# Top-k attention and a SmeLU MLP on one core: a PSUM bank for the values' result, weight words loaded ahead, two small VectorE operations moved, early MLP work limited

## The chip, the cores and the metric

The kernel runs on one core of one Trainium2 chip. The metric is the device time of one execution in microseconds (us); times of several runs are given as their median. All tensors are float32.

## The reference, cut to what matters

Attention in which each query keeps its 32 largest scores (B, H, S, D = 8, 8, 576, 64), then an MLP of 4608 tokens with 512 inputs, 2048 hidden units and the SmeLU activation.

```python
scores = scale * np.matmul(q, k.transpose(0, 1, 3, 2))        # scale = 1/sqrt(64)
kth = np.partition(scores, -top_k, axis=-1)[..., -top_k:-top_k + 1]
scores = np.where(scores >= kth, scores, -1e9)
attn = np.exp(scores - np.max(scores, axis=-1, keepdims=True))
attn = attn / (np.sum(attn, axis=-1, keepdims=True) + 1e-9)
x = np.matmul(attn, v)                                        # then (B, H, S, D) -> (B*S, H*D)

h = x @ w_in                                                  # 512 x 2048
g = np.where(h >= 1, h, np.where(h <= -1, 0.0, (h + 1) ** 2 / 4))
out = g @ w_out                                               # 2048 x 512
```

The weights w_in and w_out come as float64 and are turned into float32 on the chip from their two 32-bit words.

## The kernel before

**Steps.** Attention is cut into 144 steps. A step is one pair of heads of one tile of 128 queries (or, for the last 64 queries of a batch, two pairs of heads). `begin_at(m + 2)` makes the scores two steps ahead (L227 to L242: eight matmuls into four PSUM tiles `sp`, each copied by ScalarE into `s`). `weights` (L252 to L304) is VectorE's main work: `pairs` (L250) takes the larger of each two scores, four rounds of MAX8 (L264) and MATCH_REPLACE8 (L273) find the largest, L266 negates the first maximum for ScalarE's exponential (L268), L278 to L285 find the 32nd value `kth`, L286 notes in `excess` whether the pairing was safe, L295 masks and sums, L300 and L301 give the reciprocal, GpSimd scales (L303). `transpose_w` (L307) turns the weights by TensorE, `values` (L321) multiplies by v into the PSUM tile `po`, and ScalarE copies that into `xT` (L342, L344).

**MLP.** When the tokens of a chunk (one or two tiles) are complete, `mlp` (L353) puts its units on the list `pending`: 16 first products `hidden` (L360, into a PSUM tile `ph`), each followed by two ScalarE activations `r` and `g` (L364, L366) and three GpSimd operations (L367 to L369), then second products `final` (L377, into `py`) with the copy to `y` and the store. A unit of cost stands for 128 x 128 x 128; `hidden` costs 4 per tile, a `final` piece 8.

**PSUM.** Of eight banks, four are shared in turn by all tiles with the tag "a" (`pk`, `pkt`, `pq`, `sp`, `pw`, `pwt`, `po`), three by `ph`, one is `py`.

**Weights.** 64 pieces of 128 x 256 (32 of w_in, then 32 of w_out). `convert_piece` (L99) loads the words `raw`, shifts the high word on VectorE (L105, into `bits`), converts the low word on ScalarE (L108), and then, for even pieces, takes the sign on ScalarE (L111) and adds and multiplies on GpSimd (L112, L119); for odd pieces VectorE merges the sign bit by a mask (L123) and GpSimd adds (L125). Two pieces are begun before step 0, then one in each of the seven slots of a step, so steps 0 to 8 are "early". Afterwards `inspect_piece` (L128) loads each piece again, one a step, for a check on small values.

**Order.** TensorE, VectorE, ScalarE and GpSimd execute in the order in which the code emits (L456); each queue is in order. SyncE (SP) issues all DMAs in order. The planner `advance` (L441) emits pending MLP units when their share is due or when its own estimate of TensorE's time, `pe_time`, lies behind `now`; `K_TIME` (L438) is its estimate of VectorE's time for a step. A step's share is the work left over the steps left, at most what is pending over the steps until the next chunk.

**Keys.** `keys_of` (L185) loads two heads, transposes them, and yields, four times per batch; with the fourth it loads v. `judge` (L574) looks at all notes at the end; when a note is positive, everything is run again without pairing (it is not here).

Of the kernel before, what the change touches and what calls it, by code (L numbers as in the profile page):

```python
# [10 lines left out]
F32 = mybir.dt.float32  # L11
U32 = mybir.dt.uint32
I32 = mybir.dt.int32
AF = mybir.ActivationFunctionType
ALU = mybir.AluOpType
# [8 lines left out]
def kernel(  # L24
# [68 lines left out]
    def load_words(pool, i):  # L93
        raw = pool.tile([P, 2 * WC], U32, name="raw", bufs=3)
        nc.sync.dma_start(out=raw, in_=pieces_of_weights[i][1].bitcast(U32))
        words = raw.rearrange("p (n t) -> p n t", t=2)
        return words[:, :, 0], words[:, :, 1]

    def convert_piece(pool, i, any_size):  # L99

        lo, hi = load_words(pool, i)
        dst = pieces_of_weights[i][0]

        bits = pool.tile([P, WC], U32, name="bits", bufs=2)
# [4 lines left out]
        if any_size or i % 2 == 0:  # L109
            sign = pool.tile([P, WC], F32, name="sign", bufs=2)  # L110
            nc.scalar.activation(sign, hi.bitcast(F32), AF.Sign)  # L111
            nc.gpsimd.tensor_tensor(out=bits.bitcast(I32), in0=bits.bitcast(I32), in1=units.bitcast(I32), op=ALU.add)  # L112
            if any_size:
                size = pool.tile([P, WC], F32, name="units", bufs=3)
                nc.scalar.activation(size, hi.bitcast(F32), AF.Abs)
                nc.vector.scalar_tensor_tensor(out=sign, in0=size, scalar=TINY, in1=sign, op0=ALU.is_ge, op1=ALU.mult)

                nc.vector.tensor_scalar(bits.bitcast(F32), bits.bitcast(F32), LARGEST, -LARGEST, ALU.min, ALU.max)
            nc.gpsimd.tensor_tensor(out=dst, in0=sign, in1=bits.bitcast(F32), op=ALU.mult)  # L119
            yield  # L120
        else:
            yield
            nc.vector.scalar_tensor_tensor(out=units.bitcast(U32), in0=hi, scalar=0x80000000, in1=units.bitcast(U32),  # L123
                                           op0=ALU.bitwise_and, op1=ALU.bitwise_or)
            nc.gpsimd.tensor_tensor(out=dst.bitcast(I32), in0=bits.bitcast(I32), in1=units.bitcast(I32), op=ALU.add)  # L125
        yield

    def inspect_piece(pool, i):  # L128

        _, hi = load_words(pool, i)  # L130
# [6 lines left out]
    def run(ctx, paired):  # L137
# [47 lines left out]
        def keys_of(b):  # L185
# [4 lines left out]
            for hp in range(NHP):  # L190
# [3 lines left out]
                if hp == 0:  # L194
                    nc.sync.dma_start(out=k_tl, in_=k[b, :, SM:S, :].rearrange("h p d -> p h d"))
# [14 lines left out]
                if hp == NHP - 1:  # L210
                    got["v"], got["v_tl"] = load_values(b)
# [40 lines left out]
        def weights(st, after):  # L252
# [9 lines left out]
            for r in range(0, TOP_K, 8):  # L262
                for i in range(2):
                    nc.vector.max(out=tops[:, i, r:r + 8], in_=src[:, i, :])  # L264
                if r == 0:
                    nc.vector.tensor_scalar(nmax, tops[:, :, 0], -1.0, None, ALU.mult)  # L266
# [10 lines left out]
            if paired:  # L277
# [6 lines left out]
                for i in range(2):  # L284
                    nc.vector.max(out=kth[:, i, :], in_=tops[:, i, TOP_K - 1:TOP_K + 8])  # L285
                nc.vector.tensor_tensor(out=excess[:, 2 * m:2 * m + 2], in0=seconds[:, :, 7], in1=kth[:, :, 0],  # L286
                                        op=ALU.subtract)
# [14 lines left out]
            for i in range(2):  # L302
                nc.gpsimd.tensor_scalar(e[:, i, :], e[:, i, :], rz[:, i:i + 1], 1.0, ALU.mult, ALU.mult)  # L303
            yield  # L304
# [16 lines left out]
        def values(st):  # L321
            t, hp, v_in, v_tl = st["t"], st["hp"], st["keys"]["v"], st["keys"]["v_tl"]
            wT, wTt = st["wT"], st["wTt"]
            po = ps.tile([P, P], F32, name="po", tag="a", bufs=4)
# [28 lines left out]
        def mlp(xT, tiles, pool):  # L353
# [3 lines left out]
            def hidden(f):  # L357
# [10 lines left out]
                nc.gpsimd.tensor_tensor(out=r, in0=r, in1=r, op=ALU.mult)  # L368
# [51 lines left out]
        def convert():  # L420
# [5 lines left out]
            if begun < n_pieces:  # L426
                piece = convert_piece(mlp_pool, begun, not paired)
                next(piece)
                begun += 1

        def inspect():
            nonlocal inspected
            if paired and inspected < n_pieces:
                inspect_piece(mlp_pool, inspected)
                inspected += 1


        K_TIME, PIECE_TIME, UNIT_TIME, SLOTS = 9.8, 0.5, 0.22, 7  # L438
# [27 lines left out]
        fetch(0)  # L466
        first = keys_of(0)
        keys[0] = next(first)
        prep = None
# [28 lines left out]

        begin_at(0)
        if paired:  # L500
            pairs(state[0])
        convert_by(13.0)
        convert_by(14.0)
        next(first)
        begin_at(1)
        fetch(1)
# [12 lines left out]
        for m in range(n + 2):  # L519
# [13 lines left out]
            for slot in range(SLOTS):  # L533
# [30 lines left out]
                advance(share / SLOTS if m < n else 0.0, now)  # L564
# [52 lines left out]
```

## Time and profile before

| | us |
|---|---|
| median of 3 runs (1813.27 to 1818.81) | 1817.08 |
| the profiled execution | 1811.96 |
| its span, first to last instruction | 1810.2 |
| TensorE (PE) busy | 1667.0 (92%) |
| VectorE (DVE) busy | 1591.4 (88%) |
| ScalarE (ACT) busy | 1052.2 (58%) |
| GpSimd (POOL) busy | 938.6 (52%) |
| mean granted TensorE clock | 0.962 of full speed |

Busy times are unions of the instructions' own times; PE is the matmuls, PEld the loading of weights beside them. The ends of matmuls are modelled. The granted clock is a share of full speed (1.00 is 2.4 GHz, 0.50 is 1.2 GHz). "A <- B" in a wait says that A's engine stood idle until B was done.

### The profile page before, as it was taken

The numbers are of one execution on the slowest core, as the hardware profiler recorded it, in microseconds if no ns is written. First come the engines' busy times: TensorE is split into PE (matmuls) and PEld (weight loads), VectorE is DVE, ScalarE is ACT, GpSimd is POOL, SyncE is SP. The second block draws the span as 40 slices with busy tenths as digits, with TensorE's granted clock in tenths as the row PEclk, the third lists the DMA queues.
The fourth block names the chain that finished last, engine by engine and source line by source line (L and its number), as shares of the span: only waits on it lengthen the run. The fifth ranks groups of instructions, "written<-read, shape, count | busy, mean of one in ns | idle before, by whom it ended". The sixth has DMA issues, their size and how long they took to land.

```text
span 1810.2 us, 33204 instructions
## 1 busy us (share of the span) xinstructions
PE 1667.0 (92%) x10513; PEld 1167.9 (65%) x10513; DVE 1591.4 (88%) x5140; ACT 1052.2 (58%) x2749; POOL 938.6 (52%) x1599
## 2 busy tenths in 40 slices
PE   4476999999999999989999999989999999999998
PEld 3353677666766757556667667657676666676675
DVE  5969989989889999999997899999998799999750
ACT  5565666666666757656655555546455555465342
POOL 4685656455545635336364454527274454555453
PEclk9587999999999999999999999999999999999999
DMA  7433112111121112211111101010011000000000
GB/s 209 126 95 112 42 33 71 41 45 39 39 61 46 47 39 65 56 36 33 34 36 29 24 4 53 16 30 10 21 33 30 13 4 19 13 7 7 7 7 14
DMA packets 116667, 74.60 MB, mean 41 GB/s; under 512 B 87296, under 2 KB 95488, under 8 KB 116480
## 3 DMA queue, kind: packets, MB, share of 16 engines
q1 hardware_dynamic: 116480, 72.37, 14.1%
q8 instruction: 85, 1.39, 0.3%
q14 instruction: 102, 0.84, 0.2%
HBM read 62.91 MB, written 9.44 MB: 40 GB/s over the span
## 4 chain that ended last, share of the span: by engine, by line
PE 48%; DVE 34%; POOL 9%; ACT 4%; issue 3%; DMA 1%; POOLq 0%; SPq 0%; ACTq 0%; DVEq 0%
PE py L377 19%; PE ph L360 13%; DVE tops L264 9%; DVE more L273 8%; PE sp L239 6%; DVE e L295 5%; PE po L329 4%; PE pw L314 4%; POOL g L369 3%; POOL r L368 3%; DVE seconds L281 3%; DVE more L278 2%; DVE more L250 2%; POOL r L367 2%; POOL e L303 1%
## 5 line engine op out<-in xcount | busy, mean ns | idle before, releaser
L360 PE MATMUL ph<-xT,w_in 128*128 128x128 f32 (+1 forms) x3200 | 561.8, 331 | 5.4 <-ACT g L366 4.1
L377 PE MATMUL py<-w_out,g 128*128 128x512 f32 x1152 | 537.6, 605 | 2.5 <-ACT y L381 2.5
L360 PEld LDWEIGHTS ph<-xT,w_in 128*128 128x128 f32 x3200 | 482.1, 197 | 73.2 <-issue 31.8
L303 POOL TENSOR_SCALAR e<-e,rz 128x576 f32<-128x576 f32 x288 | 212.8, 750 | 564.2 <-DVE rz L301 528.4
L264 DVE MAX8 tops<-more 128x8 f32<-128x288 f32 x1152 | 463.2, 442 | 0.0
L273 DVE MATCH_REPLACE8 more<-tops,more 128x288 f32<-128x288 f32 x864 | 373.5, 437 | 0.0
L377 PEld LDWEIGHTS py<-w_out,g 128*128 128x128 f32 x1152 | 207.2, 192 | 225.2 <-issue 216.3
L295 DVE SCALAR_TENSOR_TENSOR e<-s,kth,e 128x576 f32<-128x576 f32 x288 | 248.6, 893 | 89.7 <-ACT e L268 43.4
L364 ACT ACTIVATE r<-ph,half 128x128 f32<-128x128 f32 (+1 forms) x400 | 167.4, 419 | 245.9 <-POOL g L369 152.0
L369 POOL TENSOR_TENSOR g<-r,g 128x128 f32<-128x128 f32 (+1 forms) x400 | 263.6, 659 | 31.4
L367 POOL TENSOR_SCALAR r<-r 128x128 f32<-128x128 f32 (+1 forms) x400 | 171.5, 429 | 176.6 <-ACT r L364 176.1
L368 POOL TENSOR_TENSOR r<-r 128x128 f32<-128x128 f32 (+1 forms) x400 | 225.3, 563 | 33.4
L242 ACT ACTIVATE s<-sp 128x288 f32<-128x288 f32 x576 | 195.9, 418 | 69.3 <-PE sp L239 39.9
L239 PE MATMUL sp<-kT,qT 64*128 64x288 f32 x1024 | 191.5, 446 | 44.0 <-ACT xT L342 35.7
L268 ACT ACTIVATE e<-s,nmax 128x576 f32<-128x576 f32 x288 | 214.9, 781 | 26.5 <-DVE nmax L266 26.2
L314 PE MATMUL pw<-ident,e 128*128 128x128 f32 x1152 | 164.1, 286 | 52.2 <-POOL e L303 50.4
L314 PEld LDWEIGHTS pw<-ident,e 128*128 128x128 f32 x1152 | 139.8, 147 | 103.9 <-POOL e L303 70.6
L315 ACT COPY wT<-pw 128x512 f32<-128x512 f32 x288 | 154.7, 594 | 28.2 <-PE pw L314 28.1
L329 PEld LDWEIGHTS po<-wT,v_in 128*64 128x64 f32 x2048 | 117.1, 142 | 82.9 <-issue 53.6
L366 ACT ACTIVATE g<-ph,minus 128x128 f32<-128x128 f32 (+1 forms) x400 | 165.5, 414 | 0.0
L239 PEld LDWEIGHTS sp<-kT,qT 64*128 64x128 f32 x1024 | 106.0, 191 | 91.2 <-ACT xT L342 47.1
L329 PE MATMUL po<-wT,v_in 128*64 128x128 f32 x2048 | 150.9, 288 | 13.9 <-ACT wT L315 13.7
(67 smaller groups left out, 1414.1 us busy)
## 6 DMA issues: line engine op xcount, KB each, us to landing
raw<-in_moe_w_in_dram SPq DMA_DIRECT2D x64, 256.0 KB, 3.0
raw<-in_moe_w_out_dram SPq DMA_DIRECT2D x64, 256.0 KB, 2.7
q_in<-in_q_dram SPq DMA_DIRECT2D x32, 256.0 KB, 3.1
k_in<-in_k_dram SPq DMA_DIRECT2D x64, 128.0 KB, 2.9
v_in<-in_v_dram SPq DMA_DIRECT2D x8, 1024.0 KB, 5.9
out_dram<-y SPq DMA_DIRECT2D x32, 256.0 KB, 2.3
k_tl<-in_k_dram SPq DMA_DIRECT2D x8, 128.0 KB, 3.2
v_tail<-in_v_dram SPq DMA_DIRECT2D x16, 64.0 KB, 2.6
```

The source lines that it names most:

```text
L239: nc.tensor.matmul(o[:, a0 - c0:a1 - c0], qT[d, g, :], kT[d, g, k0:k0 + a1 - a0], start=True, stop=True)
L264: nc.vector.max(out=tops[:, i, r:r + 8], in_=src[:, i, :])
L268: nc.scalar.activation(e[:, i, :], s[:, i, :], AF.Exp, bias=nmax[:, i:i + 1])
L273: nc.vector.match_replace(out=rest[:, i, :], in_to_replace=tops[:, i, r:r + 8], in_values=src[:, i, :], imm_value=LOWEST)
L295: nc.vector.scalar_tensor_tensor(out=e[:, i, :], in0=s[:, i, :], scalar=last[:, i:i + 1], in1=e[:, i, :], op0=ALU.is_ge, op1=ALU.mult, acc ...
L303: nc.gpsimd.tensor_scalar(e[:, i, :], e[:, i, :], rz[:, i:i + 1], 1.0, ALU.mult, ALU.mult)
L314: nc.tensor.transpose(pt[:, c, :], w[:, i, main(i)][:, c * P:(c + 1) * P], ident)
L329: nc.tensor.matmul(po[j * D:(j + 1) * D], v_in[:, h, c, :] if c < NT else v_tl[0][:, h, :], wT[:, j, c, :] if c < NT else wTt, start=(c == ...
L360: nc.tensor.matmul(ph, w_in[:, kk, f * P:(f + 1) * P], xT[:, kk, 0:cw], start=(kk == 0), stop=(kk == NK - 1))
L368: nc.gpsimd.tensor_tensor(out=r, in0=r, in1=r, op=ALU.mult)
L369: nc.gpsimd.tensor_tensor(out=g[:, 0:cw], in0=r, in1=g[:, 0:cw], op=ALU.add)
L377: nc.tensor.matmul(py, gs[f][:, i * P:(i + 1) * P], w_out[:, f, :], start=(f == 0), stop=(f == NF - 1))
```

## The change

- `po` takes its PSUM tile from the three "ph" banks instead of the four "a" banks.
- Raw words are loaded ahead: eight pieces into the still unused second buffers of `kT` and `v_in`, three into the pool's buffers, all before step 0; later pieces are loaded two ahead (conversion) or one ahead (inspection). The first keys are loaded ahead of the first queries, and `keys_of` loads one pair of heads ahead of the transposes (five yields, v with the third of four pairs).
- Four conversions instead of two are begun before step 0, ahead of its `pairs`. Mask (VectorE) conversions are the first four pieces and every fourth after; all others go by sign and multiplication. `bits` has three buffers instead of two.
- The negation (L266) moves from VectorE to ScalarE, the note in `excess` (L286) from VectorE to GpSimd, behind the scaling of e.
- While weights are converted, every second first product squares `r` on ScalarE instead of GpSimd, and at most 20 units of MLP are due per step, with no emission by `pe_time`. `K_TIME` is 9.4 instead of 9.8.

```diff
+    loaded = {}
+
+    def load(pool, i, place=None):
+        if i < n_pieces and i not in loaded:
+            loaded[i] = pool.tile([P, 2 * WC], U32, name="raw", bufs=3) if place is None else place
+            nc.sync.dma_start(out=loaded[i], in_=pieces_of_weights[i][1].bitcast(U32))
...
-        bits = pool.tile([P, WC], U32, name="bits", bufs=2)
+        bits = pool.tile([P, WC], U32, name="bits", bufs=3)
...
-        if any_size or i % 2 == 0:
+        if any_size or i % 4 < 3 and i >= 4:
...
+            k_in = load_keys(0)
+            nc.sync.dma_start(out=k_tl, in_=k[b, :, SM:S, :].rearrange("h p d -> p h d"))
+            yield got
+            for hp in range(NHP):
+                k_next = load_keys(hp + 1) if hp + 1 < NHP else None
...
-                if hp == NHP - 1:
+                k_in = k_next
+                if hp == NHP - 2:
                     got["v"], got["v_tl"] = load_values(b)
...
-                    nc.vector.tensor_scalar(nmax, tops[:, :, 0], -1.0, None, ALU.mult)
+                    nc.scalar.activation(nmax, tops[:, :, 0], AF.Copy, scale=-1.0)
...
-                nc.vector.tensor_tensor(out=excess[:, 2 * m:2 * m + 2], in0=seconds[:, :, 7], in1=kth[:, :, 0],
-                                        op=ALU.subtract)
...
+            if paired:
+                nc.gpsimd.tensor_tensor(out=excess[:, 2 * m:2 * m + 2], in0=seconds[:, :, 7], in1=kth[:, :, 0],
+                                        op=ALU.subtract)
...
-            po = ps.tile([P, P], F32, name="po", tag="a", bufs=4)
+            po = ps.tile([P, P], F32, name="po", tag="ph", bufs=3)
...
-                nc.gpsimd.tensor_tensor(out=r, in0=r, in1=r, op=ALU.mult)
+                if converted < n_pieces and f % 2:
+                    nc.scalar.activation(r, r, AF.Square)
+                else:
+                    nc.gpsimd.tensor_tensor(out=r, in0=r, in1=r, op=ALU.mult)
...
+                load(mlp_pool, begun + 1)
...
+                load(mlp_pool, inspected)
...
-        K_TIME, PIECE_TIME, UNIT_TIME, SLOTS = 9.8, 0.5, 0.22, 7
+        K_TIME, PIECE_TIME, UNIT_TIME, SLOTS, EARLY_SHARE = 9.4, 0.5, 0.22, 7, 20
...
+        room = []
+        if paired:
+            for x in (stage.tile([P, NHP, S], F32, name="kT").rearrange("p h n -> p (h n)"),
+                      stage.tile([P, H, NT, D], F32, name="v_in").rearrange("p h c d -> p (h c d)")):
+                room += [x[:, c:c + 2 * WC].bitcast(U32) for c in range(0, 8 * WC, 2 * WC)]
...
+        load_ahead(0, 2)
+        next(first)
+        load_ahead(2, 8)
+        fetch(1)
+        for i in range(len(room), len(room) + 3):
+            load(mlp_pool, i)
         begin_at(0)
+        for i in range(4):
+            convert_by(13.0)
         if paired:
             pairs(state[0])
-        convert_by(13.0)
-        convert_by(14.0)
         next(first)
         begin_at(1)
-        fetch(1)
...
-                advance(share / SLOTS if m < n else 0.0, now)
+                if early:
+                    advance(min(share, EARLY_SHARE) / SLOTS)
+                else:
+                    advance(share / SLOTS if m < n else 0.0, now)
```

## Rows read from the trace of the kernel before

**Rows 1.** Stages: stretch, busy us per engine (instructions), clock, DMA share, GB/s.
```profile
0.00:28.00 28.00, 14.54 (x48) 8.81 (x48) 11.80 (x38) 17.58 (x38) 10.79 (x26) 1.00 0.81 214
28.00:93.00 65.00, 31.40 (x173) 23.68 (x174) 60.52 (x185) 33.42 (x84) 37.97 (x53) 0.66 0.47 145
93.00:171.00 78.00, 54.70 (x308) 37.28 (x308) 62.20 (x182) 45.59 (x122) 60.16 (x97) 0.80 0.35 109
171.00:333.00 162.00, 150.36 (x1074) 109.43 (x1074) 149.93 (x494) 106.30 (x308) 88.24 (x174) 0.97 0.17 49
333.00:1745.00 1412.00, 1359.83 (x8613) 951.24 (x8612) 1303.26 (x4235) 829.66 (x2143) 712.50 (x1179) 0.98 0.11 30
```

**Rows 2.** Waits of 0 to 93, then 93 to 171 us: total, times, longest.
```profile
DVE bits L105 <- DMA raw<-in_moe_w_in_dram: 5.2, 3, 2.3
...
DVE bits L105 <- POOL w_out L125: 15.0, 7, 4.7
```

**Rows 3.** Groups by line, VectorE, 45 to 93 us: xcount | busy us, mean ns | idle.
```profile
L123 DVE SCALAR_TENSOR_TENSOR units<-raw,units 128x256 uint32<-128x256 uint32 x11 | 4.5, 409 | 0.0
...
L266 DVE TENSOR_SCALAR nmax<-tops 128x2 f32<-128x2 f32 x3 | 1.8, 591 | 0.1
```

**Rows 4.** Groups by line, VectorE, 681 to 800 us.
```profile
L286 DVE TENSOR_TENSOR excess<-seconds,kth 128x2 f32<-128x2 f32 x12 | 2.2, 182 | 0.4
L266 DVE TENSOR_SCALAR nmax<-tops 128x2 f32<-128x2 f32 x11 | 2.2, 197 | 0.4
```

**Rows 5.** Groups by line, GpSimd, 93 to 140 us.
```profile
L369 POOL TENSOR_TENSOR g<-r,g 128x128 f32<-128x128 f32 x15 | 8.1, 540 | 1.2
...
L368 POOL TENSOR_TENSOR r<-r 128x128 f32<-128x128 f32 x15 | 6.6, 438 | 1.2
L119 POOL TENSOR_TENSOR w_out<-sign,bits 128x256 f32<-128x256 f32 x8 | 6.4, 802 | 0.6
...
L367 POOL TENSOR_SCALAR r<-r 128x128 f32<-128x128 f32 x14 | 5.0, 354 | 0.0
```

**Rows 6.** Busy time in 0 to 171 us of L360, then of L377 alone.
```profile
0.00:171.00 171.00, 18.17 (x128) 16.47 (x128) 0.78 0.47 140
...
0.00:171.00 171.00, 16.59 (x28) 6.23 (x28) 0.78 0.47 140
```

**Rows 7.** Chain of waits, 857 to 863 us: start, us, what.
```profile
857.13 5.15 PE py L377 x12
```

**Rows 8.** Groups by line, TensorE, 171 to 1811 us.
```profile
L239 PE MATMUL sp<-kT,qT 64*128 64x288 f32 x936 | 171.2, 435 | 41.7 <-ACT xT L342 35.7 <-ACT xT L344 5.3 <-ACT kT L201 0.5
...
L239 PE MATMUL sp<-kT,qTt 64*64 64x288 f32 (+2 forms) x320 | 36.3, 364 | 6.5 <-ACT xT L342 6.5
```

**Rows 9.** Timeline, TensorE, then ScalarE, 397 to 404 us: start, us, [idle before].
```profile
397.63 1.09 PE L329 MATMUL po<-wT,v_in 128*64 128x128 f32 x16
...
402.90 0.75 PE L239 MATMUL sp<-kT,qT 64*128 64x288 f32 x2 [2.79 <-ACT xT L342]
...
398.86 0.36 ACT L366 ACTIVATE g<-ph,minus 128x128 f32<-128x128 f32 x1
...
402.06 0.37 ACT L364 ACTIVATE r<-ph,half 128x128 f32<-128x128 f32 x1 [1.07 <-POOL g L369]
...
402.58 0.26 ACT L342 COPY xT<-po 128x128 f32<-128x128 f32 x1
```

**Rows 10.** The stage view for 352 to 356 us.
```profile
352.00:356.00 4.00, 4.00 (x15) 3.24 (x16) 3.83 (x11) 2.51 (x8) 2.13 (x5) 0.50 0.00 0
```

**Rows 11.** Timeline, VectorE, then ScalarE, 347.5 to 353.8 us.
```profile
348.56 0.80 DVE L264 MAX8 tops<-more 128x8 f32<-128x288 f32 x2
...
353.59 0.77 ACT L268 ACTIVATE e<-s,nmax 128x576 f32<-128x576 f32 x1
```

**Rows 12.** Timeline of SP from 1.2 us; DMA issues with KB and us to landing.
```profile
1.24 1.35 SPq L193 DMA_DIRECT2D k_in<-in_k_dram  x2
...
k_in<-in_k_dram SPq DMA_DIRECT2D x64, 128.0 KB, 2.9
```

More of the change, by code (lines that the diff above doesn't have):

```diff
@@ L91, with words_of @@
                           for f in range(NF) for c in range(0, DM, WC)]
[L93 to L96, printed above, removed]
+    loaded = {}
[3 more added lines that the diff above has]
+            nc.sync.dma_start(out=loaded[i], in_=pieces_of_weights[i][1].bitcast(U32))
+    def words_of(pool, i):
+        load(pool, i)
+        words = loaded.pop(i).rearrange("p (n t) -> p n t", t=2)
         return words[:, :, 0], words[:, :, 1]
     def convert_piece(pool, i, any_size):
-        lo, hi = load_words(pool, i)
+        lo, hi = words_of(pool, i)
         dst = pieces_of_weights[i][0]
-        bits = pool.tile([P, WC], U32, name="bits", bufs=2)
+        bits = pool.tile([P, WC], U32, name="bits", bufs=3)
         nc.vector.tensor_scalar(bits, hi, 3, None, ALU.logical_shift_left)
@@ L128, in inspect_piece @@
     def inspect_piece(pool, i):
-        _, hi = load_words(pool, i)
+        _, hi = words_of(pool, i)
         for x in range(2):
@@ L189, in keys_of, with load_keys @@
             got = dict(kT=kT)
-            for hp in range(NHP):
+            def load_keys(hp):
                 k_in = stage.tile([P, NT, 2, D], F32, name="k_in")
@@ L193, in keys_of @@
                     nc.sync.dma_start(out=k_in[:, :, j, :], in_=whole(k, b)[:, 2 * hp + j])
-                if hp == 0:
-                    nc.sync.dma_start(out=k_tl, in_=k[b, :, SM:S, :].rearrange("h p d -> p h d"))
+                return k_in
+            k_in = load_keys(0)
[3 more added lines that the diff above has]
+                k_next = load_keys(hp + 1) if hp + 1 < NHP else None
                 pt = ps.tile([P, NT, P], F32, name="pk", tag="a", bufs=4)
@@ L464, in fetch, with load_ahead @@
                 q_ins[rounds[i]] = load_queries(*rounds[i])
-        fetch(0)
+        room = []
[3 more added lines that the diff above has]
+                room += [x[:, c:c + 2 * WC].bitcast(U32) for c in range(0, 8 * WC, 2 * WC)]
+        def load_ahead(i0, i1):
+            for i in range(i0, min(i1, len(room))):
+                nc.sync.dma_start(out=room[i], in_=pieces_of_weights[i][1].bitcast(U32))
+                loaded[i] = room[i]
         first = keys_of(0)
         keys[0] = next(first)
+        fetch(0)
         prep = None
```

## The prediction

> **What bounds the kernel now.** I read the stage table first [rows 1], because shares over the whole span mix two regimes. Up to 171 us (steps 0 to 8, in which weight pieces are converted) TensorE is idle 70 of 171 us (28 − 14.5, 65 − 31.4 and 78 − 54.7) and its granted clock is 0.66 and 0.80 in the last two stretches: VectorE paces 28 to 93 us (60.5 of 65 busy), and from 93 to 171 GpSimd does (60.2 of 78, while VectorE stands 15.0 us at its shift because the buffer is still GpSimd's [rows 2]). From 171 us on TensorE is busy 93% and then 96%, VectorE 93% and 92%: TensorE is the bound on average, VectorE where a step carries little MLP work. What TensorE loses there is one thing: before the scores' matmuls it is idle 41.7 + 6.5 us, released by ScalarE's copy of xT [rows 8]. After such a stop the clock falls to its lower level (0.50, 1.2 GHz, over 352 to 356 us, right behind such a stop [rows 10]).
>
> **The change, part by part**, against the profiled execution's 1811.96 us.
>
> *Early stage, loads and start.* Removed: VectorE's waits for raw words, 5.2 us [rows 2]. Added: eleven pieces (2.9 MB) now stand on SP's queue ahead of the later queries, of the third and fourth k_in and of v_in, against three before. At the 214 GB/s of the first stretch [rows 1], eight more pieces of 256 KB push k_in of pair 2 back by some 10 us, to about 20 us, where its transposes (and ScalarE's kT copies, with everything behind them on that in-order engine) may stand 2 to 4 us. Two more conversions precede the first pairs operation, with three mask operations of 0.41 us [rows 3], each behind a ScalarE conversion, so the first top-k starts about 1.3 us later; that work is saved afterwards. Taken −4 us, bounds −7 and +4.
>
> *Early stage, VectorE.* The negation is 0.59 us and a mask operation 0.41 us a piece here [rows 3]. Of 64 pieces 19 instead of 32 take the mask path. In the four steps from 28 to 93 us that is 4 × 0.59 = 2.4 for the negation, 4 × 0.18 = 0.7 for the subtraction [rows 4], and about 7 × 0.41 = 2.9 for masks: −6. GpSimd gets 13 more multiplications of 0.80 us [rows 5], about six of them in this stretch, beside VectorE's work while GpSimd is at 58%. I take −4, bounds −6 and +2.
> In these rows the same negation of 2 columns costs 0.59 us, and 0.20 us where nothing is converted [rows 3, 4]. The Trainium skill (SBUF — State Buffer, Who interferes with whom) says that VectorE in a two-port mode, as tensor_scalar can be, and GpSimd exclude each other for a whole instruction. These two rows agree; the shifts, also tensor_scalar, would then meet more GpSimd work than now, and by this rule the −4 would be about −2.
>
> *Early stage, MLP.* I worked the planner's loop through with the old and the new numbers; its old result is what the trace holds (128 matmuls of first products and 28 of second ones by 171 us [rows 6], 64 and 56 units, as it says). Old: 28, 44, 24, 8 and 16 units in steps 4 to 8, all sixteen first products of a chunk within steps 4 and 5. New: 0, 16, 20, 20 and 24. Sixteen first products are 16 × (0.35 + 0.44 + 0.54) = 21 us of GpSimd [rows 5], on top of conversions: that made VectorE's 15.0 us of waiting. Spread over steps 5 to 8 it is 5.3 us a step, less 2 × 0.44 where ScalarE squares every second one; conversions are 7 × (0.75 × 2 + 0.25) × 0.80 = 9.8, two scalings of e, taken like a multiplication, 1.6: together some 16 us against steps of 78/4 = 19.5. A third bits buffer takes more of the wait. Taken −10, bounds −15 and 0. What is late next is GpSimd again, not far behind VectorE. Early sum −18.
>
> *Steps 9 to 22.* The planner pays the 40 units back: 432 instead of 392. A unit is 5.15/24 = 0.215 us [rows 7], so +8.6 us in the stage where TensorE is 93% busy, less some 5 us of the stops below. Taken +4, bounds 0 and +9. From step 22 on both planners keep nothing pending and emit nearly the same units in each step, K_TIME notwithstanding.
>
> *Values' bank.* With po out of the four "a" banks, each step takes seven there and no scores wait for xT. The wait goes to the three "ph" banks: po needs the one whose g copy is three back. Example [rows 9]: values begin at 397.63, the scores stop 2.79 us for the xT copy of 402.58, behind three pairs of r and g. The bank that po would need is free at 398.86 + 0.36 = 399.22, so the values begin 1.6 us later and the scores end near 402.5 instead of 403.65: 1.1 of 2.79 us saved. The same reading of every stop (the 41.7 and 6.5 us [rows 8]) gives 12 us of new waits and TensorE going on 34 us earlier in sum, of which 5 are counted in steps 9 to 22 and 5 lie in steps that VectorE paces. Of the other 24 I take 19, since in those steps ScalarE and GpSimd are near their limit; bounds 0 and 34. The lower clock level: 0.98 over 1412 us [rows 1] is 28 us lost; most stops vanish or shrink, so I take about a third of it back: −8, bounds 0 and −25.
>
> *VectorE and the small operations, from step 23.* Removed are 0.20 and 0.18 us a step [rows 4], overlapping their neighbours, so about 0.27 in start-to-start time. It counts where VectorE paces: 36 steps with 22 to 27 units in the planner's list, −9; bounds −3 and −25 (some 95 more steps at part of it). Price of the new places: on ScalarE 0.26 us a step by the nearest row (a copy of 128 columns [rows 9]), 58% busy there, ahead of exp, so exp is later by up to 0.2: I take +3, bounds 0 and +20 (0.16 in each of 121 steps). On GpSimd at most the 0.35 of a small r [rows 5], half idle: 0, bounds 0 and +5.
>
> **Sum:** −18 + 4 − 19 − 8 − 9 + 3 = −47 from 1811.96: **1765 us**. The three timed runs have a median of 1817, 5 us above the profiled one; I leave 1765.
>
> **Rivals.**
> *A. The bank moves the stop, no more.* In steps of first products GpSimd's three operations for each pace ScalarE, and ScalarE TensorE; then TensorE only waits at another bank. For it: the r just ahead of the example's xT copy had itself waited 1.07 us for GpSimd [rows 9]. Against: from 333 to 1745 us GpSimd is busy 50% and TensorE 96% [rows 1]. Without the 19 and 8: 1792.
> *B. The early stage stays GpSimd's.* Sixteen microseconds a step is still above VectorE's own; more multiplications and ScalarE in order behind the new squares (16/2 of them) may keep it at today's time. Early sum −4 in place of −18: 1779, or 1783 with 9 instead of 4 repaid.
> *C. More than forecast.* All 24 and 25 us of the clock, VectorE's 15: 1737.
> *D. Not what it says:* the bank moves the stop and the early gain is repaid: 1812 − 4 + 9 − 9 + 3 = 1811.
> *E. Slower.* The negation moves to an engine that is far behind: ScalarE's exp began at 353.59, when VectorE's second round of maxima, which writes other columns of the same tops tile, had begun at 348.56 [rows 11]. If that round had to wait until ScalarE has read columns 0 and 40 between which it writes, it would stand 353.59 + 0.26 − 348.56 = 5.3 us in such a step; it decides at 47/5.3, nine such steps, and with half of the 144 the time is 1765 + 380 = 2145. Against it: two loads into interleaved halves of one k_in tile were issued within 1.35 us though one takes 2.9 us to land [rows 12], so regions with strides are told apart.
>
> **Chances.** Forecast 0.54 (its own range 1745 to 1778), A 0.18, B 0.12, C 0.09, D 0.04, E 0.03. Range 1735 to 1798: from C to A with the sum of B's doubt on it; D and E and a little of C lie outside. A measurement here tells 0.3%, 5.4 us, from no change. Faster 0.93 (forecast, A, B, C), same 0.04 (D), slower 0.03 (E).
>
> **What would show it.** Early: end of step 8 (its subtraction, now on GpSimd; use the second tops round) near 153 instead of 171; no VectorE wait for raw words in the first 45 us; VectorE's wait for GpSimd's w_out below 5 us. Bank: no row of scores released by xT; instead po rows released by ScalarE's g, about 12 us; clock 0.99 from 333 us on. VectorE: steps of 10.3 us where there were 10.56. Wrong if scores or values keep 40 us of idle time, if TensorE's second stage (171 to 333 us before) grows by over 9 us, if VectorE's maxima are released by ScalarE (E), or if pk waits for k_in over 4 us.

## The result, and the profile after

The changed kernel takes **1768.4 us** (median of 4 runs, 1768.0 to 1768.5), beside 1815.4 us for the kernel before on the same chip: a ratio of 0.974, with a 95% interval of 0.972 to 0.976. Its profiled execution took 1768.54 us (span 1766.6), 43.4 us less than that of before. TensorE's mean granted clock rose from 0.962 to 0.976.

As in the prediction, stretches are cut at the ends of steps: a step ends with VectorE's second search for the 32nd score (before L285, after L298). The stage view of after, with the columns of [rows 1]; the cuts are after steps 0, 4, 8, 22 and 143:

```profile
0.00:28.00 28.00, 14.53 (x48) 8.94 (x48) 14.65 (x39) 19.41 (x43) 12.63 (x28) 1.00 0.85 232
28.00:91.00 63.00, 26.38 (x152) 19.87 (x152) 57.42 (x171) 36.94 (x95) 44.58 (x62) 0.70 0.52 154
91.00:168.00 77.00, 46.67 (x306) 38.73 (x308) 59.08 (x167) 47.73 (x135) 61.85 (x99) 0.80 0.34 102
168.00:328.00 160.00, 149.69 (x1084) 106.73 (x1081) 141.57 (x463) 105.06 (x315) 87.43 (x186) 0.99 0.17 46
328.00:1703.00 1375.00, 1336.69 (x8625) 929.57 (x8623) 1251.40 (x3993) 844.65 (x2269) 745.20 (x1300) 1.00 0.11 31
1703.00:1767.00 64.00, 56.20 (x303) 37.47 (x303) 3.71 (x12) 19.87 (x60) 29.05 (x75) 0.96 0.03 11
```

| | before, us | after, us | difference | forecast |
|---|---|---|---|---|
| end of step 8 | 170.9 | 167.7 | −3.2 | −18 |
| steps 9 to 22 | 161.9 | 160.1 | −1.8 | +4 |
| steps 23 to 143 | 1412.2 | 1375.3 | −37.0 | −33 (19 + 8 + 9 − 3) |
| behind step 143 | 65.1 | 63.5 | −1.6 | none |

So the total came out near the forecast, with an early stage that gave little and a late one that gave more. The early stage itself shows where its gain went. VectorE's timeline of after: the two searches for the 32nd score in each of steps 4 to 8, and in two neighbouring steps of the late stage (start, us):

```profile
90.54 0.24 DVE L298 MAX8 kth<-tops 128x8 f32<-128x9 f32 x2
104.42 0.24 DVE L298 MAX8 kth<-tops 128x8 f32<-128x9 f32 x2
123.28 0.24 DVE L298 MAX8 kth<-tops 128x8 f32<-128x9 f32 x2
146.05 0.24 DVE L298 MAX8 kth<-tops 128x8 f32<-128x9 f32 x2
167.47 0.24 DVE L298 MAX8 kth<-tops 128x8 f32<-128x9 f32 x2
...
770.57 0.24 DVE L298 MAX8 kth<-tops 128x8 f32<-128x9 f32 x2
780.74 0.24 DVE L298 MAX8 kth<-tops 128x8 f32<-128x9 f32 x2
```

Before, steps 4 to 8 ended at 92.8, 117.6, 139.1, 154.8 and 170.9 us; now at 90.8, 104.7, 123.5, 146.3 and 167.7. By step 6 the kernel is 15.6 us ahead, close to what was forecast, and then steps 7 and 8 take 22.8 and 21.4 us where they took 15.6 and 16.1. Much of that lead is work put off: by the end of step 6 TensorE had done 96 units of MLP before and has done 32 now (counted from the matmuls of both traces), and what is put off comes in steps 7 to 22. The two late lines show a shortest step of 10.17 us, where the shortest took 10.52.

What stands in those two steps shows in the waits of 28 to 168 us (total, times, longest):

```profile
ACT r L383 <- POOL r L381: 18.5, 8, 3.8
DVE units L129 <- ACT units L114: 12.6, 8, 3.0
...
DVE bits L111 <- POOL w_out L131: 4.0, 2, 3.5
```

The wait of [rows 2] for GpSimd's w_out fell from 15.0 to 4.0 us as forecast, and two others took its place: ScalarE before its new squares (L383), and VectorE behind ScalarE's conversion of the low words (L114). From 168 us to the end, TensorE's five largest groups (busy, mean ns of one, idle and its releasers):

```profile
L374 PE MATMUL ph<-xT,w_in 128*128 128x128 f32 (+1 forms) x3072 | 538.9, 328 | 17.1 <-ACT g L380 15.1
L394 PE MATMUL py<-w_out,g 128*128 128x512 f32 x1144 | 528.0, 600 | 2.0 <-ACT y L398 2.0
L252 PE MATMUL sp<-kT,qT 64*128 64x288 f32 x934 | 146.9, 433 | 0.0
L328 PE MATMUL pw<-ident,e 128*128 128x128 f32 x1088 | 145.2, 275 | 15.6 <-ACT s L255 6.6 <-POOL e L314 5.4 <-POOL g L386 2.7
L343 PE MATMUL po<-wT,v_in 128*64 128x128 f32 x1920 | 132.8, 280 | 13.2 <-ACT g L380 12.8
```

The idle time ahead of the scores, 41.7 us in [rows 8], is gone; the values (po) now stand idle 13.2 us, nearly all of it for ScalarE's g, and the first products (ph), which share their banks, 17.1. The busy time of the scores' matmuls fell from 171.2 to 146.9 us at the same mean of one (435 and 433 ns): less of it is the run-up of groups that stops break into pieces, as the two matmuls behind a stop in [rows 9] (0.75 us for x2) against 1.24 us for x8 in one piece after.

### The profile page after: what moved, and what is told of

Read it like the earlier page. It is cut to its first block, busy times and chain, and to the rows that moved or that the text cites. A ratio compares the mean times of both kernels' runs of the same rounds, so it can differ in the third digit from the quotient of the medians.

```text
span 1766.6 us, 33273 instructions
## 1 busy us (share of the span) xinstructions
PE 1630.2 (92%) x10513; PEld 1141.3 (65%) x10513; DVE 1527.8 (86%) x4839; ACT 1073.7 (61%) x2914; POOL 980.8 (56%) x1748
## 4 chain that ended last, share of the span: by engine, by line
PE 61%; POOL 14%; DVE 13%; ACT 5%; issue 4%; DMA 1%; SPq 0%; POOLq 0%; DVEq 0%; ACTq 0%
PE py L394 24%; PE ph L374 16%; PE sp L252 7%; PE po L343 6%; PE pw L328 5%; POOL g L386 4%; POOL r L385 3%; DVE tops L277 3%; DVE e L306 3%; DVE more L286 3%; POOL e L314 3%; POOL r L381 2%; DVE seconds L294 1%; ACT s L255 1%; DVE more L291 1%
## 5 line engine op out<-in xcount | busy, mean ns | idle before, releaser
L374 PE MATMUL ph<-xT,w_in 128*128 128x128 f32 (+1 forms) x3200 | 559.9, 328 | 17.1 <-ACT g L380 15.1
L394 PE MATMUL py<-w_out,g 128*128 128x512 f32 x1152 | 531.8, 600 | 2.0 <-ACT y L398 2.0
L374 PEld LDWEIGHTS ph<-xT,w_in 128*128 128x128 f32 x3200 | 475.8, 193 | 88.5 <-ACT g L380 30.7
L286 DVE MATCH_REPLACE8 more<-tops,more 128x288 f32<-128x288 f32 x864 | 375.8, 443 | 0.0
L378 ACT ACTIVATE r<-ph,half 128x128 f32<-128x128 f32 (+1 forms) x400 | 167.5, 419 | 226.2 <-POOL g L386 170.7
L386 POOL TENSOR_TENSOR g<-r,g 128x128 f32<-128x128 f32 (+1 forms) x400 | 263.8, 659 | 34.2 <-ACT r L383 2.5
L381 POOL TENSOR_SCALAR r<-r 128x128 f32<-128x128 f32 (+1 forms) x400 | 181.4, 454 | 151.9 <-ACT r L378 151.8
L385 POOL TENSOR_TENSOR r<-r 128x128 f32<-128x128 f32 (+1 forms) x392 | 221.2, 564 | 32.7
L252 PE MATMUL sp<-kT,qT 64*128 64x288 f32 x1024 | 167.5, 443 | 3.4 <-ACT kT L213 2.7
L356 ACT COPY xT<-po 128x128 f32<-128x128 f32 x128 | 34.1, 267 | 207.3 <-PE po L343 207.1
```

What stands on the lines that cost most here:

```text
L252: nc.tensor.matmul(o[:, a0 - c0:a1 - c0], qT[d, g, :], kT[d, g, k0:k0 + a1 - a0], start=True, stop=True)
L286: nc.vector.match_replace(out=rest[:, i, :], in_to_replace=tops[:, i, r:r + 8], in_values=src[:, i, :], imm_value=LOWEST)
L374: nc.tensor.matmul(ph, w_in[:, kk, f * P:(f + 1) * P], xT[:, kk, 0:cw], start=(kk == 0), stop=(kk == NK - 1))
L381: nc.gpsimd.tensor_scalar(r, r, 1.0, 0.0, ALU.min, ALU.max)
L386: nc.gpsimd.tensor_tensor(out=g[:, 0:cw], in0=r, in1=g[:, 0:cw], op=ALU.add)
L394: nc.tensor.matmul(py, gs[f][:, i * P:(i + 1) * P], w_out[:, f, :], start=(f == 0), stop=(f == NF - 1))
```

## The experiments

Medians and ratios to the kernel before on the same chip; the last three columns come from the profiled execution of each, cut as above. The kernel before itself read 1815.4 to 1818.4 us from chip to chip, so between kernels of different rows 2 to 3 us are near the limit of what can be told. The columns come from one execution each: step 8 ends at 167.4 to 167.7 us in the kernels that leave the early stage alone (after, e1, e12), and steps 23 to 143 take 1375.3 to 1378.4 us in those that leave the late work alone (after, e3, e5, e6, e7, e9, e11).

| | median, us | ratio, 95% | step 8 ends | steps 9–22 | steps 23–143 |
|---|---|---|---|---|---|
| before | 1815.4 | 1 | 170.9 | 161.9 | 1412.2 |
| after | 1768.4 | 0.972–0.976 | 167.7 | 160.1 | 1375.3 |
| e1, bank undone | 1809.5 | 0.994–0.998 | 167.6 | 171.1 | 1408.4 |
| e2, bank alone | 1788.1 | 0.982–0.986 | 171.5 | 160.1 | 1389.2 |
| e3, no ScalarE squares | 1764.8 | 0.970–0.973 | 161.1 | 160.7 | 1376.3 |
| e4, both small operations undone | 1777.1 | 0.976–0.979 | 167.5 | 160.4 | 1383.7 |
| e5, early limit undone | 1766.3 | 0.969–0.974 | 169.4 | 154.2 | 1378.4 |
| e6, masks for all odd pieces | 1765.8 | 0.969–0.972 | 162.6 | 160.4 | 1377.2 |
| e7, e3 and e6 | 1761.1 | 0.967–0.971 | 158.8 | 161.2 | 1375.5 |
| e8, negation undone | 1772.4 | 0.973–0.977 | 166.9 | 160.2 | 1379.3 |
| e9, e7 and e5 | 1765.1 | 0.969–0.973 | 167.8 | 152.6 | 1378.0 |
| e10, bank and small operations alone | 1776.8 | 0.975–0.979 | 170.3 | 159.9 | 1378.7 |
| e11, no raw words ahead | 1774.0 | 0.974–0.978 | 170.7 | 160.8 | 1376.3 |
| e12, K_TIME undone | 1777.4 | 0.975–0.980 | 167.4 | 160.6 | 1385.6 |

### The values' bank: undone (e1), and alone (e2)

e1 is the changed kernel with

```diff
-            po = ps.tile([P, P], F32, name="po", tag="ph", bufs=3)
+            po = ps.tile([P, P], F32, name="po", tag="a", bufs=4)
```

> The changed kernel with the values' result back in one of the four shared banks, all else as changed. Theory 1 (the bank is the main gain: it takes TensorE's stops at the scores and the lower clock level behind them): the stops for xT come back, 40 to 50 us of idle time at the scores, the clock after 328 us falls from 1.00 to about 0.98, and the time is 1768 + about 34 = 1802 us (1794 to 1810). Rival A (the bank only moves the stop): 1768 to 1773 us, TensorE's total idle time unchanged within 5 us.

Measured: 1809.5 us (10 runs, 1798 to 1814), 41 us above the changed kernel, all of it from step 9 on: 11.0 us in steps 9 to 22 and 33.2 in steps 23 to 143 of the profiled execution. As the first theory has it, the stops are back at the scores, and the clock is back at 0.98. TensorE's group of scores from 168 us, then the stage view (with the stretches of after; step 22 of e1 ends at 338.7):

```profile
L252 PE MATMUL sp<-kT,qT 64*128 64x288 f32 x936 | 172.4, 437 | 39.9 <-ACT xT L356 34.1 <-ACT xT L358 5.6
```

```profile
168.00:328.00 160.00, 147.91 (x1028) 108.15 (x1027) 131.80 (x426) 99.50 (x295) 84.14 (x183) 0.94 0.15 45
328.00:1747.00 1419.00, 1376.29 (x8688) 962.32 (x8686) 1263.14 (x4030) 859.95 (x2290) 741.73 (x1303) 0.98 0.11 30
```

Without the bank, everything else in the change gives 6 us. e2 is the kernel before with the same line changed the other way.

> The kernel before with the values' result in a bank of the first products, and nothing else changed. Theory 1: no idle time at the scores for xT, 10 to 30 us at the values and first products instead, clock from 333 us on at 0.99 or more, time 1815 - 36 = 1779 us (1772 to 1787); early stage as before, so step 8's second maxima end within 2 us of the kernel before. Rival A: 1810 to 1816 us. If the gain needs the lighter VectorE step as well (both must shrink together), the time lies between, 1790 to 1805 us.

Measured: 1788.1 us, a ratio of 0.984 (0.982 to 0.986), 27.6 us less. That lies between the two bands expected. So the bank is most of the change by itself, and worth 41 with the rest beside it. What it does is not what the forecast said. The last stage of e2, and what TensorE waits for in it (total, times, longest):

```profile
333.00:1721.00 1388.00, 1335.89 (x8586) 927.51 (x8584) 1301.70 (x4234) 821.77 (x2142) 720.85 (x1180) 1.00 0.11 30
```

```profile
PE ph L360 <- ACT g L366: 12.4, 19, 2.2
PE pw L314 <- ACT s L242: 11.2, 8, 3.1
PE pw L314 <- POOL e L303: 10.3, 12, 1.5
PE po L329 <- ACT g L366: 8.1, 8, 1.7
```

From step 23 on TensorE is idle 1388.0 − 1335.9 = 52.1 us; before it was 1412.0 − 1359.8 = 52.2 [rows 1]. The idle time moved, all of it: to the first products, the transposes and the values. The 24 us between these two views (23.0 by the ends of the steps, since step 22 of e2 ends at 331.6) are in TensorE's busy time. Most of them stand in the scores, whose group in these stretches is, before and in e2:

```profile
L239 PE MATMUL sp<-kT,qT 64*128 64x288 f32 x840 | 151.9, 435 | 35.1 <-ACT xT L342 31.2 <-ACT xT L344 3.8
```

```profile
L239 PE MATMUL sp<-kT,qT 64*128 64x288 f32 x834 | 130.5, 431 | 0.0
```

The busy time of this group falls by 21.4 us while one matmul is as long as before. Most of that isn't the clock: if each matmul is counted from the end of the one before it, the scores that ran at a clock of 1.00 took 138.2 us before (830 of them) and take 121.7 in e2 (832). I read these 16.5 us as the price of starting a group again behind a stop (22 stops ahead of these scores before, none in e2). That is argued from matmul ends that are modelled, and no run broke the scores up without a stop. What is left of the 23, some 6 us, is the clock's, less what new stops cost the groups behind them. The granted clock by itself could account for at most 17: its shortfall from 1.00, summed over stretches of 2 us in this stage, is 22.2 us before and 5.1 in e2 (some of it in idle stretches, where it costs nothing). What changed with it is how the idle time is split up. Before, twelve stops of 1.5 us or more make 32.5 us and three of them are over 4 us; in e2 nine make 17.6, and the longest is 3.1; in the changed kernel there are three. TensorE's waits before, in the same stage, and its timeline around the stretch of [rows 10]:

```profile
PE sp L239 <- ACT xT L342: 34.4, 20, 4.6
```

```profile
351.92 1.32 PE L239 MATMUL sp<-kT,qT 64*128 64x288 f32 x2 [4.25 <-ACT xT L342]
353.17 3.64 PE L360 MATMUL ph<-xT,w_in 128*128 128x128 f32 x16
...
357.63 1.95 PE L360 MATMUL ph<-xT,w_in 128*128 128x128 f32 x16
```

Sixteen matmuls of the same kind take 3.64 us at the lower level and 1.95 us four microseconds later: a stop of 4.25 us costs 1.7 us more in this block alone. That fewer long stops are what keeps the clock up is argued from these rows; no run varied the length of a stop alone.

### The two small operations: both undone (e4), one undone (e8), added to the bank (e10)

e4, the changed kernel with the negation and the note back on VectorE; e8 has only the first line of it:

```diff
-                    nc.scalar.activation(nmax, tops[:, :, 0], AF.Copy, scale=-1.0)
+                    nc.vector.tensor_scalar(nmax, tops[:, :, 0], -1.0, None, ALU.mult)
...
+                nc.vector.tensor_tensor(out=excess[:, 2 * m:2 * m + 2], in0=seconds[:, :, 7], in1=kth[:, :, 0],
+                                        op=ALU.subtract)
...
-            if paired:
-                nc.gpsimd.tensor_tensor(out=excess[:, 2 * m:2 * m + 2], in0=seconds[:, :, 7], in1=kth[:, :, 0],
-                                        op=ALU.subtract)
```

> The changed kernel with both small operations back on VectorE (negation and note). The forecast's terms: VectorE's 9 us come back, ScalarE's 3 us go, and 1 to 3 us come back in the early stage, so 1775 to 1778 us. Theory 3 (from 168 us on TensorE is busy 97% at full clock and VectorE waits 109 us for ScalarE's exponential, so a shorter VectorE step only waits longer): 1767 to 1771 us, with that wait falling to 60 to 80 us.

> The changed kernel with the negation back on VectorE, the note staying on GpSimd. Both back cost 8.7 us. If each is worth its VectorE time, half of it: 1771 to 1774 us. If ScalarE's 0.2 us ahead of every exponential costs as much as VectorE saves (its waits for the exponential are 109 us with the change, 43 before), then the negation is worth nothing there and the note all: 1766 to 1769 us, and VectorE's wait for the exponential below 80 us.

Measured: 1777.1 us for e4 and 1772.4 for e8, so +8.7 for both and +4.0 for the negation; step 8 ends within 0.9 us of the changed kernel's, and the difference is in steps 23 to 143 (8.4 and 4.0 us). The price of the new places can be seen in the idle time of VectorE ahead of its masked sum, which needs the exponential; the groups of the whole span, first after, then e4 (the last figures are the idle time and what ended most of it):

```profile
L306 DVE SCALAR_TENSOR_TENSOR e<-s,kth,e 128x576 f32<-128x576 f32 x288 | 246.5, 885 | 111.0 <-ACT e L281 108.8
```

```profile
L308 DVE SCALAR_TENSOR_TENSOR e<-s,kth,e 128x576 f32<-128x576 f32 x288 | 253.5, 911 | 63.0 <-ACT e L281 24.7
```

From 168 us on VectorE's busy time is 56 us less than in e4 (1396.7 against 1452.9). It stands 48 us more ahead of this operation, and the kernel is 8.7 us faster: in most of these steps VectorE isn't the bound, and a shorter VectorE only waits longer there. So the theory by which these moves gain nothing falls. No search for maxima on VectorE is released by ScalarE in any stage of after; rival E has no row.

e10 is the kernel before with the bank of e2 and both small operations moved.

> The kernel before with the values' bank and both small operations moved, nothing else. The bank alone gave 1788 us, and with all else the small operations gave 8.7 us. If the two help each other (the bank was worth 41 us when it was undone beside the small operations, 28 us alone), 1772 to 1777 us. If they only add, 1778 to 1782 us.

Measured: 1776.8 us, 11.4 less than e2. These two parts add up to 39 of the 47 us (40.9 against the kernel before on e10's own chip). The time lies 0.2 us inside the band of parts that help each other; beside the 8.7 of e4 this is too little to tell that they do. TensorE's idle time from step 23 on is where the 11 us come from: 1378.7 − 1337.4 = 41.3 us, against 52.1 in e2.

### The early stage: squares (e3), limit (e5), masks (e6), and together (e7, e9)

e3 gives all squares back to GpSimd:

```diff
-                if converted < n_pieces and f % 2:
-                    nc.scalar.activation(r, r, AF.Square)
-                else:
-                    nc.gpsimd.tensor_tensor(out=r, in0=r, in1=r, op=ALU.mult)
+                nc.gpsimd.tensor_tensor(out=r, in0=r, in1=r, op=ALU.mult)
```

> The changed kernel with all squares of r on GpSimd, none on ScalarE. Theory 2 (in steps 6 to 8 ScalarE, in order, stands 13 us at the eight squares for GpSimd's r, and VectorE's masks stand some 10 us for the conversions queued behind them): VectorE's wait for units falls from 12.6 us to under 4, step 8 ends 5 to 9 us earlier than the 167.7 us of the changed kernel, time 1759 to 1764 us. Rival (GpSimd paces these steps, and gets 8 x 0.44 = 3.5 us more): step 8 ends 0 to 4 us later, time 1768 to 1773 us.

Measured: 1764.8 us, and step 8 ends at 161.1 instead of 167.7. The 18.5 us of ScalarE's waiting are gone with the squares, and so is most of VectorE's behind it; of e3, 28 to 168 us:

```profile
DVE units L129 <- ACT units L114: 2.5, 4, 1.3
```

So the squares cost 6.6 us of the early stage. How they do it is seen in the timeline of after, 153 to 156 us, GpSimd, ScalarE and VectorE:

```profile
153.01 0.72 POOL L118 TENSOR_TENSOR bits<-bits,units 128x256 int32<-128x256 int32 x1
153.81 0.72 POOL L125 TENSOR_TENSOR w_out<-sign,bits 128x256 f32<-128x256 f32 x1
154.50 0.29 POOL L381 TENSOR_SCALAR r<-r 128x128 f32<-128x128 f32 x1
154.83 0.31 ACT L383 ACTIVATE r<-r 128x128 f32<-128x128 f32 x1 [3.63 <-POOL r L381]
155.04 0.51 ACT L114 ACTIVATE units<-raw,two 128x256 f32<-128x256 uint32 x1
...
155.58 0.42 DVE L129 SCALAR_TENSOR_TENSOR units<-raw,units 128x256 uint32<-128x256 uint32 x1 [2.96 <-ACT units L114]
```

The square needs GpSimd's r, and that r is queued behind, among others, the two operations of a piece's conversion, 0.72 us each. ScalarE is in order: it stands 3.63 us at a square of 0.31 us, and the conversion of the next piece's low words stands behind it, which VectorE waits for another 2.96 us. Of the final time 3.6 us came through, between what the theory and the rival gave: steps 9 to 22 and 23 to 143 were 0.6 and 1.0 us longer.

e5 lifts the limit, with `advance(share / SLOTS if m < n else 0.0, now)` in early steps too.

> The changed kernel with the early MLP emitted by share and estimate again, without the limit of 20 units (and its second squares on ScalarE as changed). Forecast's view: sixteen first products crowd into steps 4 and 5, GpSimd paces, step 8 ends 8 to 12 us later than the 167.7 us of the changed kernel, and 8.6 us of MLP are not repaid later, so 1768 to 1773 us in sum. Rival (the limit gains nothing early, since steps 7 and 8 took 21 to 23 us with it, and it only defers work into the stage that TensorE bounds): step 8 ends within 3 us, time 1759 to 1764 us.

Measured: 1766.3 us, 2 us below the changed kernel and between the two times expected; the step's end is where the rival has it. The limit is worth nothing there. It brings step 8 forward by 1.7 us (169.4 to 167.7), and steps 9 to 22 pay 5.9 for it (154.2 to 160.1).

e6 has masks for all odd pieces as before, 32 instead of 19:

```diff
-        if any_size or i % 4 < 3 and i >= 4:
+        if any_size or i % 2 == 0:
```

> The changed kernel with masks for every odd piece as before (32 by mask on VectorE, 32 by sign and multiplication on GpSimd) instead of 19 and 45. If GpSimd paces the early steps (busy 62 of 77 us from 91 to 168 us), 13 multiplications of 0.8 us fewer bring step 8 forward by 4 to 9 us, time 1760 to 1766 us. If VectorE paces them, 13 masks of 0.41 us more put it back by 3 to 6 us, time 1770 to 1775 us. If ScalarE's stops at the squares pace them, nothing moves, 1767 to 1770 us.

Measured: 1765.8 us, with step 8 at 162.6, 5.1 us earlier. Taking masks from VectorE did not pay, as the theory of a late GpSimd has it. The run doesn't show GpSimd's part alone: each of the 13 pieces gave GpSimd a multiplication and ScalarE a sign (0.43 us in after), and ScalarE was late too, behind its squares. With the squares gone as well (e3 to e7, below) the masks are worth 2.3 us.

e7 joins e3 and e6:

> The changed kernel with squares on GpSimd and masks for every odd piece, both as before. With the squares on GpSimd alone step 8 ended at 161.1 us and the time was 1764.8 us. If GpSimd paces what is left, step 8 ends at 154 to 158 us and the time is 1757 to 1762 us; if VectorE paces it, 163 to 167 us and 1766 to 1770 us.

Measured: **1761.1 us** (1759.8 to 1763.9), a ratio of 0.969 (0.967 to 0.971), the fastest of all kernels here and 7 us below the changed one. Step 8 ends at 158.8, 12.1 us earlier than before and just behind the band for a GpSimd that paces what is left. e9 is e7 without the limit:

> The changed kernel with squares on GpSimd, masks for every odd piece, and no limit on the early MLP, all three as before, so that of the change the bank, the loads ahead, the third bits buffer, the two small operations and K_TIME remain. It was 1761.1 us with the limit. If the limit only defers work, step 8 ends 2 to 8 us later than the 158.8 us there but the time is 1756 to 1762 us. If without it GpSimd's crowding of steps 4 and 5 is not made good, 1763 to 1768 us.

Measured: 1765.1 us, step 8 at 167.8. With the squares and the masks out of the way the limit does bring its gain, 9.0 us by step 8, and 8.6 of it is paid back in steps 9 to 22 (152.6 to 161.2), which is what 40 units at the price of [rows 7] come to. So the limit defers work at nearly no gain (0.4 us); of the 4.0 us between e7 and e9, 2.5 lie in steps 23 to 143, within what such kernels differ by there.

### Words ahead (e11) and K_TIME (e12)

e11 loads no raw words ahead (neither the eleven before step 0 nor one or two pieces later):

```diff
-                load(mlp_pool, begun + 1)
...
-                load(mlp_pool, inspected)
...
-        if paired:
+        if False:
             for x in (stage.tile([P, NHP, S], F32, name="kT").rearrange("p h n -> p (h n)"),
...
-        for i in range(len(room), len(room) + 3):
-            load(mlp_pool, i)
```

> The changed kernel with no raw words loaded ahead: each piece is loaded where it is converted or inspected, as before; keys still come one pair ahead. Forecast's view: 4 us come back in steps 0 and 1, 1771 to 1775 us, with 3 to 6 us of VectorE waits for raw words in the first 45 us. Rival (VectorE's wait of 7.7 us for the first piece and 4.2 us for later ones in the changed kernel show that eleven loads ahead push others back, so nothing is gained): 1765 to 1770 us.

Measured: 1774.0 us, +5.5. Step 0 ends 4.1 us later (32.4 instead of 28.3) and step 8 3.0 us later. VectorE's waits for raw words, 0 to 45 us:

```profile
DVE bits L111 <- DMA raw<-in_moe_w_in_dram: 14.3, 4, 10.1
```

In the changed kernel the one such wait in that stretch is that for the first piece, 7.7 us, in which VectorE has nothing else to do; the wait of 10.1 here is the same one with the words further back in SP's queue, and the other 4.2 us are in the forecast's 3 to 6. Behind it the changed kernel isn't free of them: from 28 to 168 us VectorE waits 5.7 us for raw words, 2.8 in e11. Four conversions still stand ahead of the first step in e11, with their words late, so 5.5 is the price of taking the loads from this kernel; before, with two conversions there, the waits were 5.2 us in all [rows 2].

e12 has 9.8 for K_TIME, in the changed kernel.

> The changed kernel with K_TIME 9.8 as before; worked through, 24 of the 144 steps then get other units or another place for them. Forecast's view: worth nothing, 1766 to 1771 us. If K_TIME explains why the changed kernel with both small operations back gained 5 us over the bank alone after step 8, 1772 to 1777 us.

Measured: 1777.4 us, +9.0, where my sum held this number for nothing. The whole loss is in three places, steps 23 to 38 (+3.4 us), 78 to 87 (+3.2) and 107 to 114 (+3.6); elsewhere the differences cancel out. Worked through with both values, the planner emits the first products in another order just there: with 9.8 and the new early part a chunk's 64 units fall as 32 and 32 over two steps (23 and 24, for example), with 9.4 as 36 and 28, and so does the kernel before with 9.8. TensorE's timeline around step 23, first e12, then after:

```profile
340.85 1.16 PE L374 MATMUL ph<-xT,w_in 128*128 128x128 f32 x8 [0.20 <-ACT g L380]
344.95 1.98 PE L343 MATMUL po<-wT,v_in 128*64 128x128 f32 x16 [2.95 <-ACT g L380]
```

```profile
342.41 1.16 PE L374 MATMUL ph<-xT,w_in 128*128 128x128 f32 x8 [0.63 <-ACT g L380]
343.69 1.09 PE L343 MATMUL po<-wT,v_in 128*64 128x128 f32 x16
```

In e12 the values meet the bank of a g that comes late, stand 2.95 us, and then run at the lower level (granted clock 0.50 from 345 to 349 us; 1.98 us for what takes 1.09). So 9.0 us is the price of undoing K_TIME in this kernel, not what it brings against the kernel before, whose own split was the good one: e10, with 9.8, needs 1378.7 us for steps 23 to 143, 6.9 less than e12. Nor does K_TIME explain why e4 is 5.5 us shorter than e2 in these steps: from step 25 on nearly every step of these two has the same first products. That stays open.

## Why the prediction was right, and where its steps failed

The time forecast (1765) and the time measured (1768) are 3 us apart. That they are so near is in part luck: errors in the steps stood against each other.

**Early loads and start: right in kind, the size not shown.** Forecast −4. Step 0 ends 0.3 us later than before and step 4 2.0 earlier, with all early parts in it; undone in the changed kernel, the loads cost 3.0 us by step 8 and 5.5 in all (e11). SP's queue in front of k_in shows as forecast: the transposes of the third pair stand 2.3 us for it until 19.8 us (forecast 2 to 4, at about 20).

**Early VectorE: wrong in the masks.** The step costed the masks that left VectorE as a gain (2.9 of the 6) and the multiplications that GpSimd got as hidden. Undone, the masks bring step 8 forward by 5.1 us (e6), or 2.3 where the squares are undone too (e7). The cover named, GpSimd at 58%, is an average of 28 to 93 us; in the steps that followed, GpSimd's queue was what ScalarE and VectorE waited for. The signs that ScalarE got with these pieces had no term at all.

**Early MLP: the step that failed.** Forecast −10 of an early sum of −18; the sum came to −3.2. The limit itself was costed rightly: 9.0 us by step 8 where nothing else is in its way (e9 to e7), and rows up to step 6 are 15.6 us ahead, though with 64 units less done. GpSimd's work in steps 5 to 8 was sized rightly too, 4 × 16 us and 61.9 measured, but the four steps took 76.9 us for it. The squares were the miss. They stood in the sum as 2 × 0.44 us saved on GpSimd in each step, with no price on the engine that got them and nothing named that queues behind them there. Their price is a wait, not a duration: 18.5 us in 8 squares, and 6.6 us of step 8's end. Rival B, the early stage staying GpSimd's, named ScalarE in order behind the new squares; for this stage B was the better account, and its −4 is nearly what came. The squares and the masks together are 8.9 us of the 14.8 that did not come (e7); the other 5.9 stay open.

**Steps 9 to 22: the repayment right, the rest too small.** The repayment was forecast as 8.6 and is 8.6 (e9 to e7), or 5.9 in the changed kernel (e5). The other part, forecast as −5, is 154.2 − 161.9 = −7.7: e5 against before, both with the early MLP unlimited. Of this the bank alone gives 1.8 (e2) and with the small operations 2.0 (e10). What brings the remaining 5.7 stays open: e11 and e12 each move this stage by less than 1 us. The parts don't simply add here, for in the changed kernel, with its 40 units more, undoing the bank costs this stage 11.0 us (e1).

**Values' bank and clock: the sum right, the terms not.** The forecast had −19 of stops and −8 of clock from step 23 on. Alone the bank brings 23 us there and 27.6 in all. The term of 19, TensorE going on earlier, is not what came: the idle time does not fall at all. In its place stand 16.5 us of scores that are no longer broken into pieces, for which the sum had no term, and some 6 of the clock, where 8 was forecast. Rival A said that the bank moves the stop and no more. For the idle time that is what the rows show; A's time (1792) was wrong because it gave up the 8 of the clock together with the 19, and because it too had nothing for the broken scores. New waits at the values were forecast as 12 us and are 13.2 + 2.0; the idle time at the first products, 17.1 where it was 4.2, was not seen in the forecast, though they take the same three banks.

**VectorE and the small operations: right.** Forecast −9 and +3. Undone, +8.7 (e4); added to the bank, −11.4 (e10). The shortest step fell by 0.35 us, from 10.52 to 10.17, where 0.27 was counted. Rival E is refuted by the rows, and D and C by the time.

**K_TIME: the term right, the reason wrong.** The sum held it for nothing. The sentence "nearly the same units" is true of the two kernels it compares: from step 25 on the matmuls of first products fall on the same steps in both traces, but for two places. "K_TIME notwithstanding" is what fails. With the new early part it is the 9.4 that keeps the split of before; with 9.8 the split is 32 and 32 instead of 36 and 28, which costs some 3 us in each of three places, where it meets a late bank (e12).

Against the sum, then: 14.8 us of the early stage that did not come, 5.8 less to pay in steps 9 to 22, 4.0 more from step 23 on and 1.6 behind the last step, which no term held. That leaves the 3.5 us between 1765 and the profiled 1768.54.

## What to carry to other kernels

Before an operation moves to an engine that is half idle, look at what it must wait for there and what is queued behind it: a square of 0.31 us held an in-order ScalarE for up to 3.8 us, and VectorE behind it. Where a tile of the critical matmuls shares its PSUM banks with one that is copied out late, count not the idle time alone but which group each stop breaks up, how long it is, and at which clock TensorE runs behind it; here the same 52 us of idle time went with 23 us less of busy time. An estimate in a planner is a change of order: work the order through for every step that it changes, and don't take its price from undoing it alone.

## What the runs showed of the hardware that was not expected

Some two-input operations of VectorE grew longer in steps in which GpSimd had more work (19.8 of 32 us busy in the first stretch below, 34.2 of 44.5 in the second). VectorE's groups by line, 139 to 171 us before (first fence) and 123.5 to 168 us after:

```profile
L295 DVE SCALAR_TENSOR_TENSOR e<-s,kth,e 128x576 f32<-128x576 f32 x4 | 3.1, 810 | 0.0
```

```profile
L306 DVE SCALAR_TENSOR_TENSOR e<-s,kth,e 128x576 f32<-128x576 f32 x4 | 4.7, 1207 | 0.0
...
L129 DVE SCALAR_TENSOR_TENSOR units<-raw,units 128x256 uint32<-128x256 uint32 x4 | 2.3, 564 | 9.6 <-ACT units L114 9.6
```

The masked sum went from a mean of 810 to 1207 ns, and the mask operation, 409 ns in [rows 3], took 564. The search for maxima, with one input, stays at 443 ns in both. But two other two-input groups, of two instances each, didn't grow: the smaller of each two scores (L278, now L291) is at 746 ns in both, and the minimum into tops (L282, now L295) went from 296 to 174. These are a few instances in one execution of each kernel. From 123 to 168 us the masked sum is at 813 ns in e9 (GpSimd busy 31.3 of 45 us) and at 1045 in e7 (35.1). The Trainium skill (SBUF — State Buffer, Who interferes with whom) says that a VectorE instruction with two inputs in SBUF contends with a GpSimd instruction that reads SBUF. The rows of the masked sum and of the mask agree in direction, and no run here separates this from other causes.

The other surprise is what equal idle time can hide: at 52.2 and 52.1 us of it in the last stage, TensorE's busy time fell by 23 us and the granted clock went from 0.98 to 1.00 when one bank was changed (e2).
